# A matrix product by 15 products in place of 11 per two chunks, and one list that orders all engines

## The chip, the cores and the metric

The kernel runs on one core of one Trainium2 chip. The metric is the device time in microseconds (us) of one execution; lower is better. One core has five engines that run side by side, each through its own instructions in order: TensorE (PE, matrix products; its weight loads are listed apart as PEld), VectorE (DVE), ScalarE (ACT), GpSimd (POOL) and SyncE (SP, which here only issues DMAs).

## What is computed

```python
# x: (8, 4096, 192), weight: (8 heads, 7 taps)
w = exp(weight - max) / sum                # softmax over the taps
out[b, s, h, :] = sum_k w[h, k] * x_padded[b, s + k, h, :]   # causal, 6 zeros ahead
X = out.reshape(32768, 192)
h = X @ w_in                               # w_in:  (192, 2048)
g = h * sigmoid(h)                         # SiLU
result = g @ w_out                         # w_out: (2048, 192)
```

All is fp32 (the weights arrive as float64 and are rounded in the kernel). Nearly all arithmetic is in the two products, h and the result.

## The kernel before, in words

The 32768 tokens are worked in 32 blocks of 1024 tokens, each in two halves of 512 (n = 0, 1). Data lie transposed, channels on partitions, tokens along the free dimension. The 192 channels are three thirds of 64; the 2048 columns of `w_in` are 16 chunks of 128. A product of one third of the channels, one chunk and one token half is a matmul with 64 rows: it takes half of the PE array, so two such matmuls, one on the upper rows and one on the lower, run at once. I call the time of such a pair a slot. Block 0 is worked by plain products (`up_plain`, `down_plain`) while the weights are prepared; blocks 1 to 31 use schemes that save products.

**h, blocks 1 to 31 (`product`, line 476 on).** The 16 chunks form 8 pairs m. For a pair, two thirds of the channels and two token halves make eight ordinary products; a Strassen-like scheme does them with seven (P1 to P7), of differences of the tokens (`win`, line 429 on, four per block, on DVE) and of sums of the weights (`combine_in`, on POOL, once). The last third of the channels adds four plain ones (E11, E12, E21, E22). That is 11 of 64 rows for a pair, 88 for a block: 44 slots. The products accumulate in three PSUM banks per pair (`"1"`, `"b"`, `"d"`). Bank `"1"` grows by one product at a time, and its value on the way is copied out (`s1`, `s3` on ACT, `s2` on DVE, line 512), so that the next product onto it waits for the copy. DVE then adds a copy and another bank into g (C11, C22, C12, line 521), and ACT takes SiLU (lines 516 and 518).

**The result (`sum_g`, `out_slot`, `merge`, `turn_out`).** A seven-product scheme over channel halves and token halves. `sum_g` (line 538) makes four differences of g for each j of four, 16 DVE instructions of 1024 columns per block; `out_slot` (line 570) issues four matmuls of 128 rows by 32 columns at once, 48 times per block, eight of them only 128 columns wide: 42 slots' worth. `merge` (lines 630 to 650) puts the six accumulators together, `turn_out` transposes and stores.

**The convolution.** For the next block, DVE transposes the input (`turn_in`, line 387) and does seven taps for each of three thirds (`conv`, lines 406 and 409). `spread` copies each third by DMA to both halves of the partitions (`dup`), where the matmuls read it.

**What sets the order.** The string `PLAN` is written out by hand or by a planner outside the kernel: entries between bars are slots, tokens name instructions (P, E products; s, C, g sums and SiLU; v conv taps; t sums of g; w differences of tokens; M, x, y, z merging; a minus sign means the previous block). `pin` keeps every engine's instructions in the order of issue. In the plan before, 44 slots are all h, then come the slots of the result (`down`), so a block has a stage of h and a stage of the result. PSUM has eight banks, handed out by a pool.

Of the kernel before, what the change touches and what calls it, by code (L numbers as in the profile page):

```python
# [17 lines left out]
def kernel(  # L18
# [54 lines left out]
    upool = ctx.enter_context(tc.tile_pool(name="up", bufs=13))  # L73
# [8 lines left out]
        "P1.0 P1.1 -x1.0 -M4.0 | P1.2 P5.0 -M5.0 s1.1 -M7.0 | P5.1 E22.0 s1.0 -o.1 s1.2 | "  # L82
        "E22.1 P6.1 -o.2 | P6.0 P1.3 s2.1 | P6.2 P5.2 -o.3 s1.3 s2.0 | P5.3 P7.1 s2.2 | "
        "P7.0 E22.2 i.0 s3.1 | P7.2 P6.3 i.1 s3.0 C22.1 | E22.3 E21.1 s3.2 s2.3 | "
        "P4.0 P4.1 g22.1 C22.0 | E12.1 P7.3 C22.2 g22.0 | E21.0 E12.0 i.2 C21.1 s3.3 | "
        "E21.2 E12.2 C21.0 C22.3 | P3.1 P3.0 g22.2 | P4.2 P4.3 g22.3 C12.0 | "
        "E12.3 P2.0 C12.1 g12.0 | P2.1 E11.0 v.00 C21.2 v.01 g12.1 | E11.1 E21.3 C11.0 | "
        "P1.4 P1.5 v.02 C21.3 | P1.6 P3.2 g11.0 C11.1 s1.4 | P3.3 P5.4 C12.2 s1.5 | "
        "P6.4 E22.4 s1.6 C12.3 g11.1 | P5.5 P6.5 s2.4 g12.2 | E22.5 P1.7 v.03 g12.3 s2.5 | "
        "P7.4 P2.2 s1.7 v.04 | P6.6 E11.2 s3.4 v.05 | P2.3 P7.5 C22.4 | "  # L90
        "P4.4 P6.7 s2.6 s3.5 C11.2 | E11.3 E12.4 g22.4 s2.7 g11.2 | P7.6 E21.5 C22.5 | "
        "E21.4 P7.7 C11.3 s3.6 | P3.5 P4.5 v.06 g22.5 s3.7 t.00 | E21.6 P3.4 C21.4 | "
        "E12.5 P4.7 C21.5 t.01 | P4.6 P2.4 g11.3 C12.4 | P5.7 E11.4 C21.6 C12.5 | "
        "E22.7 E21.7 g12.4 C11.4 g12.5 | P2.5 P5.6 C22.7 C21.7 | E11.5 E22.6 t.03 g11.4 | "
        "E12.7 P2.6 g22.7 C22.6 | P3.7 E11.6 C11.5 g22.6 | P2.7 E12.6 t.02 g11.5 | "
        "E11.7 P3.6 C11.6 | C12.7 g11.6 | C11.7 g12.7 C12.6 | g11.7 v.10 g12.6 | v.11 | "
        "v.12 | v.13 v.14 | v.15 | v.16 | t.10 | . | t.11 | . | . | t.13 | v.20 t.12 | . | "
        "v.21 | v.22 | v.23 | v.24 v.25 | v.26 | t.20 | . | . | t.21 | . | t.23 | t.22 | "
        "t.30 | . | t.31 | w.0 | t.32 | . | t.33 | . | w.1 | w.2 | z1.0 w.3 | y0.0 | y1.0 | "
        ". | y2.0 M1.0 | M2.0 | M6.0 | x0.0 | M3.0 x2.0 | o.0"  # L100
# [19 lines left out]
    def load(b, ks=range(NK)):  # L120
        if b not in nats:
            nats[b] = xpool.tile([P, NK, TB // SQ, SQ], F32, tag="nat", name="nat")
        nat = nats[b]
        for k in ks:
            for i in range(P // SQ):
                c = R * k + SQ * (i % 2)
                queue = nc.scalar if not b and k == 0 and i % 2 == 0 else nc.sync
                ins = queue.dma_start(
                    out=nat[SQ * i : SQ * i + SQ, k, :, :],
                    in_=x_v[2 * b + i // 2][:, :, c : c + SQ],  # L130
                )
                if not b:
                    pin(ins)
# [175 lines left out]
    def combine_in(j):  # L309


        s, r = ws[j], wr[j]
        comb(s[:, 1, 0, :], s[:, 1, 0, :], s[:, 1, 1, :], ALU.add)
        comb(s[:, 0, 0, :], s[:, 0, 0, :], s[:, 1, 0, :], ALU.subtract)
        comb(s[:, 0, 0, :], s[:, 0, 0, :], s[:, 0, 1, :], ALU.add)
        comb(s[:, 1, 1, :], s[:, 0, 2, :], s[:, 1, 2, :], ALU.subtract)
        comb(r[:, 0, 1, :], r[:, 1, 0, :], r[:, 1, 1, :], ALU.add)
        comb(r[:, 0, 1, :], r[:, 0, 1, :], r[:, 0, 0, :], ALU.subtract)
        comb(r[:, 1, 0, :], r[:, 0, 0, :], r[:, 1, 0, :], ALU.subtract)
# [58 lines left out]
    def turn_in(b, k):  # L378
        if k == 0 and b:
            xt = xts[b] = xpool.tile([P, NK, pad + TB], F32, tag="xt", name="xt")  # L380
            if b * TT % S == 0:
                nc.gpsimd.memset(xt[0:R, :, 0:pad], 0.0)
            else:
                nc.gpsimd.tensor_copy(xt[0:R, :, 0:pad], tails.pop(b))
        xt = xts[b]
        pin(
            nc.vector.transpose(
                xt[:, k, pad : pad + TB], nats[b][:, k, :, :].rearrange("p k c -> p (k c)")
            )
        )  # L390
        if k == NK - 1:
            if b:
                nc.sync.dma_start(out=xt[R:P, :, 0:pad], in_=xt[0:R, :, TB : TB + pad])
            if (b + 1) * TT % S:
                tails[b + 1] = xpool.tile([R, NK, pad], F32, tag="tail", name="tail", bufs=2)
                nc.sync.dma_start(out=tails[b + 1], in_=xt[R:P, :, TB : TB + pad])
# [16 lines left out]

    def spread(b, k):

        if b not in dups:
            dups[b] = xpool.tile([P, 2, NK, TB], F32, tag="dup", name="dup")
        src = nats[b][:, k, :, :].rearrange("p k c -> p (k c)")
        for n in range(2):
            for e in range(2):  # L420
                nc.sync.dma_start(
                    out=dups[b][R * e : R * e + R, n, k, :], in_=src[R * n : R * n + R, :]
                )
# [3 lines left out]
    def win(b, i):  # L427

        d = dups[b]
        if i == 0:  # L430
            wins[b] = xpool.tile([P, 4, TB], F32, tag="win", name="win")
        t = wins[b]
        u, v = (
            (d[:, 1, 0, :], d[:, 0, 0, :]),
            (d[:, 1, 1, :], t[:, 0, :]),
            (d[:, 1, 1, :], d[:, 1, 0, :]),
            (d[:, 0, 1, :], t[:, 1, :]),
        )[i]
        pin(nc.vector.tensor_tensor(t[:, i, :], u, v, op=ALU.subtract))
# [35 lines left out]
    def product(b, m, name):  # L475
        d, t = dups[b], wins[b]
        e, r, s = m % 2, wr[m // 2], ws[m // 2]

        other, bn, w, v = {
            "P1": (0, "1", r[:, 0, 0, :], d[:, 0, 0, :]),  # L480
            "P6": (0, "1", r[:, 0, 1, :], t[:, 1, :]),
            "P7": (0, "1", r[:, 1, 0, :], t[:, 2, :]),
            "P4": (0, "1", r[:, 1, 1, :], t[:, 3, :]),
            "E21": (0, "1", r[:, 1, 2, :], d[:, 0, 2, :]),
            "P2": (1, "b", s[:, 0, 1, :], d[:, 0, 1, :]),
            "E11": (1, "b", s[:, 0, 2, :], d[:, 0, 2, :]),
            "P5": (1, "d", s[:, 1, 0, :], t[:, 0, :]),
            "E22": (1, "d", s[:, 1, 2, :], d[:, 1, 2, :]),
            "P3": (1, "d", s[:, 0, 0, :], d[:, 1, 1, :]),
            "E12": (1, "d", s[:, 1, 1, :], d[:, 1, 2, :]),  # L490
        }[name]
        half = e ^ other
        first = (b, m, bn) not in bk
        if first:
            bk[b, m, bn] = bank()
        pin(
            nc.tensor.matmul(  # L497
                bk[b, m, bn], rows(w, half), rows(v, half), start=first, stop=True,
                skip_group_check=True,
# [3 lines left out]
    def g_of(b, m, a, n):  # L503
        return g_tile(b, m // 2, a)[:, n, m % 2, :]

    def sums_h(b, name, m):


        if name[0] == "s":
            u = us[b, m, name[1]] = upool.tile([P, TB], F32, tag="u", name="u")  # L510
            copy = nc.vector.tensor_copy if name == "s2" else nc.scalar.copy
            pin(copy(u, bk[b, m, "1"]))  # L512
            return
        g = g_of(b, m, int(name[1]) - 1, int(name[2]) - 1)
        if name == "C21":
            pin(nc.scalar.activation(g, bk[b, m, "1"], AF.Silu))
        elif name[0] == "g":
            pin(nc.scalar.activation(g, g, AF.Silu))  # L518
        else:
            i, bn = {"C11": ("1", "b"), "C22": ("3", "d"), "C12": ("2", "d")}[name]  # L520
            pin(nc.vector.tensor_tensor(g, us.pop((b, m, i)), bk[b, m, bn], op=ALU.add))  # L521

    def sum_g(b, j, i):
# [14 lines left out]
        pin(nc.vector.tensor_tensor(t[i // 2][:, i % 2, :], u, v, op=ALU.subtract))  # L538

    def out_slot(b, j, i, e, half=None):  # L540
# [4 lines left out]
        g = [gs[b, j, a] for a in range(2)]  # L545
        w, x_ = wo[j], wx[j]
        at = 6 if i == 3 and half else i
        if at not in accs.setdefault(b, {}):
            accs[b][at] = bank()

        def t(k):
# [4 lines left out]
            1: lambda: (a_[0][0], g[0][:, 0]),  # L556
            2: lambda: (a_[0][1], g[1][:, 0]),
            3: lambda: (x_[:, 2], g[1][:, 1]),
# [6 lines left out]
        for q in range(4):  # L565
# [8 lines left out]
                    start=j == 0 and e == 0,  # L574
                    stop=j == NJ - 1 and e == 1,
# [3 lines left out]

    def down(b, j):  # L580

        for i in (0, 1, 2, 4, 3, 5) if j < NJ - 1 else (0, 1, 2, 3, 5, 4):
            for e in range(2):
                for half in range(2) if i == 3 and b == NB - 1 else (None,):
                    out_slot(b, j, i, e, half)
                yield
        for a in range(2):
            del gs[b, j, a]
# [324 lines left out]
```

## Time and profile before

The time is 2409.25 us (median of 3 runs, 2409.24 to 2409.34). The profiled execution spans 2407.7 us.

| | us |
|---|---|
| PE busy | 2400.0 of 2407.7 |
| DVE busy | 2062.1 |
| ACT busy | 994.2 |
| POOL busy | 71.0 |
| start until block 1 (plain products, weights) | 101.4 |
| h of one block (176 matmul records) | 37.97 |
| result of one block (384 records) | 36.22 |

An fp32 matmul leaves two records in the trace, one for each pass, so 88 products are 176 records. "Busy" of an engine is the union of its instructions' time; the mean duration of a group is that of one instruction from its start to its end, and consecutive DVE or ACT instructions overlap a little, so that two of them in a row start closer together than one lasts. A wait is shown as idle time before an instruction, with the engine and line that ended it. The chain that ended last is followed back from the last instruction of the program and tells which engine set the end.

### The profile page before, as it was taken

Reading aid. Unit: us, or ns where it says so; the run is one execution under the profiler, and the core shown is the slowest. Engines: PE = TensorE matmul, PEld = TensorE weight load, DVE = VectorE, ACT = ScalarE, POOL = GpSimd, SP = SyncE. Lnnn points to the kernel's source line nnn. Section 1 sums busy time; section 2 is a strip of 40 time slices with the busy share of each in tenths; the row PEclk is TensorE's granted clock in tenths of the full one; section 3 lists DMA queues with packets and bytes.
Section 4 is the critical chain, followed back from the end, with each engine's and each line's share of the span. In section 5 each row is a group of like instructions: output and inputs, shape, how many; then the busy total and the mean of one; then the engine's idle time right before and its main releaser. Section 6 shows DMA issues by size and latency. Waiting matters only on the chain.

```text
span 2407.7 us, 43335 instructions
## 1 busy us (share of the span) xinstructions
PE 2400.0 (100%) x17878; PEld 942.8 (39%) x17878; DVE 2062.1 (86%) x2812; ACT 994.2 (41%) x1873; POOL 71.0 (3%) x99
## 2 busy tenths in 40 slices
PE   9999999999999999999999999999999999999998
PEld 4333443334433344433344333443334433334433
DVE  8789888888888898888988888888889888898876
ACT  4334543334533345433454334453334533345432
POOL 4300000000000000000000000000000000000000
PEclk9999999999999999999999999999999999999999
DMA  7322122221222222222222222122222222222220
GB/s 160 60 45 47 34 36 54 54 41 32 44 46 54 40 41 36 45 54 44 45 37 36 54 51 43 32 39 51 53 41 40 36 45 54 43 43 37 38 40 14
DMA packets 453718, 110.59 MB, mean 46 GB/s; under 512 B 424080, under 2 KB 429200, under 8 KB 453520
## 3 DMA queue, kind: packets, MB, share of 16 engines
q1 hardware_dynamic: 449872, 105.85, 24.0%
q8 instruction: 140, 2.29, 0.4%
q0 software_dynamic: 448, 1.58, 0.3%
q10 hardware_dynamic: 3200, 0.39, 0.1%
q14 instruction: 58, 0.48, 0.1%
HBM read 31.46 MB, written 25.17 MB: 24 GB/s over the span
## 4 chain that ended last, share of the span: by engine, by line
PE 100%; DVE 0%; ACT 0%; issue 0%; ACTq 0%
PE ps L497 49%; PE ps L570 47%; PE ps L599 2%; PE ps L460 2%; PE ps L805 1%; PE ps L339 0%; DVE cmb L111 0%; ACT u L111 0%; DVE osb L111 0%; PE ps L365 0%; ACTq L739 0%; DVE zeros L111 0%; DVE warm L111 0%; ACTq L111 0%
## 5 line engine op out<-in xcount | busy, mean ns | idle before, releaser
L497 PE MATMUL ps<-dup,ws 64*128 64x512 f32 x2480 | 869.9, 589 | 0.0
L570 PE MATMUL ps<-g,wo 128*32 128x512 f32 x2976 | 661.8, 593 | 0.0
L521 DVE TENSOR_TENSOR g<-u,ps 128x512 f32<-128x512 f32 x744 | 486.1, 681 | 119.2 <-PE ps L497 89.8
L497 PE MATMUL ps<-win,wr 64*128 64x512 f32 x1488 | 567.7, 589 | 0.0
L570 PE MATMUL ps<-t,wo 128*32 128x128 f32 (+2 forms) x4528 | 500.6, 446 | 0.0
L518 ACT ACTIVATE g<-g 128x512 f32<-128x512 f32 x744 | 444.6, 630 | 97.3 <-DVE g L521 97.3
L497 PEld LDWEIGHTS ps<-dup,ws 64*128 64x128 f32 x2480 | 363.3, 187 | 291.8 <-issue 277.7
L570 PE MATMUL ps<-t,wx 128*32 128x512 f32 x2976 | 452.7, 592 | 0.0
L409 DVE SCALAR_TENSOR_TENSOR nat<-xt,taps,nat 128x512 f32<-128x512 f32 x564 | 423.4, 751 | 18.3 <-ACT nat L404 3.7
L497 PE MATMUL ps<-dup,wr 64*128 64x512 f32 x992 | 420.0, 596 | 0.0
L512 ACT COPY u<-ps 128x512 f32<-128x512 f32 x496 | 277.7, 588 | 229.3 <-PE ps L497 226.2
L638 ACT COPY cmb<-ps 96x512 f32<-96x512 f32 x30 | 17.4, 581 | 805.3 <-PE ps L570 805.3
L538 DVE TENSOR_TENSOR t<-g 128x1024 f32<-128x1024 f32 x248 | 299.9, 1220 | 27.2 <-PE ps L570 27.2
L538 DVE TENSOR_TENSOR t<-g,t 128x1024 f32<-128x1024 f32 x248 | 303.2, 1223 | 13.6 <-PE ps L570 3.2
L497 PEld LDWEIGHTS ps<-win,wr 64*128 64x128 f32 x1488 | 233.6, 187 | 175.3 <-issue 147.0
L570 PEld LDWEIGHTS ps<-t,wo 128*32 128x32 f32 x4528 | 180.4, 110 | 219.7 <-issue 199.5
L497 PE MATMUL ps<-win,ws 64*128 64x512 f32 x496 | 242.2, 589 | 0.0
L570 PE MATMUL ps<-g,wx 128*32 128x512 f32 x1488 | 234.6, 592 | 0.0
L570 PEld LDWEIGHTS ps<-t,wx 128*32 128x32 f32 x2976 | 121.9, 110 | 278.8 <-issue 269.5
L650 DVE TENSOR_TENSOR cmb<-cmb,ps 96x512 f32<-96x512 f32 x150 | 102.2, 682 | 135.2 <-ACT u L635 133.1
L497 PEld LDWEIGHTS ps<-dup,wr 64*128 64x128 f32 x992 | 160.6, 187 | 128.1 <-issue 114.2
L570 PEld LDWEIGHTS ps<-g,wo 128*32 128x32 f32 x2976 | 168.6, 110 | 98.3 <-issue 98.3
(72 smaller groups left out, 1225.6 us busy)
## 6 DMA issues: line engine op xcount, KB each, us to landing
dup<-nat SPq DMA_DIRECT2D x376, 128.0 KB, 2.3
nat<-in_x_dram SPq DMA_DIRECT2D x382, 64.0 KB, 2.4
out_dram<-osb SPq DMA_DIRECT2D x376, 64.0 KB, 2.0
raw<-in_moe_w_out_dram SPq DMA_DIRECT2D x8, 384.0 KB, 3.9
raw<-in_moe_w_in_dram SPq DMA_DIRECT2D x12, 192.0 KB, 4.7
ws<-wr POOLq DMA_DIRECT2D x8, 192.0 KB, 4.3
raw<-in_moe_w_in_dram SPq DMA_DIRECT2D x6, 128.0 KB, 3.3
xt<-xt SPq DMA_DIRECT2D x31, 4.5 KB, 1.9
```

The source lines that it names most:

```text
L409: nc.vector.scalar_tensor_tensor(out=dst, in0=src, scalar=tap, in1=dst, op0=ALU.mult, op1=ALU.add)
L460: nc.tensor.matmul(hs[a, n, e], rows(wr[j], e)[:, a, k, :], rows(d, e)[:, n, k, :], start=k == 0, stop=k == NK - 1,)
L497: nc.tensor.matmul(bk[b, m, bn], rows(w, half), rows(v, half), start=first, stop=True, skip_group_check=True,)
L512: pin(copy(u, bk[b, m, "1"]))
L518: pin(nc.scalar.activation(g, g, AF.Silu))
L521: pin(nc.vector.tensor_tensor(g, us.pop((b, m, i)), bk[b, m, bn], op=ALU.add))
L538: pin(nc.vector.tensor_tensor(t[i // 2][:, i % 2, :], u, v, op=ALU.subtract))
L570: nc.tensor.matmul(accs[b][at][SQ * q : SQ * q + SQ, to], lhs[:, e, SQ * k : SQ * k + SQ], rhs[:, e, ts(q, TB // 4) if i == 5 else to], st ...
L599: nc.tensor.matmul(acc[k][R * n : R * n + R, :], wo[j][:, a, e, R * k : R * k + R], gs[b, j, a][:, n, e, :], start=j == 0 and a == 0 and e ...
L638: pin(nc.scalar.copy(c[0], acc[0][0:n, :]))
L650: pin(nc.vector.tensor_tensor(out_, u, v, op=ALU.add))
L805: nc.tensor.matmul(by_pe[k][n], rows(diag, n)[:, k, i, :], rows(xts[0], n)[:, k, i : i + TB], start=i == 0, stop=i == K - 1,)
```

## The change

For h, three chunks are taken together with all three channel thirds and both token halves: 18 ordinary products become 15. Five groups of three chunks cover 15 of the 16 chunks; the sixteenth is done plainly (`plain`, three products of 64 rows for one token half, six of half the columns for the other). So a block has 75 + 3 + 3 = 81 half-array products of 512 columns in place of 88. In a group, products run in three chains of accumulation, each on one bank: (5, 2, 6, 1, 0, 14), (3, 9, 7, 4, 8) and (12, 10); 13 and 11 are added by PE onto banks that DVE wrote. The first chain's value is copied out by ACT (`u`) after five of its six products; DVE makes two sums from PSUM into PSUM (`X`), three into g (`a`) and two corrections in place (`b`); ACT does SiLU of six (`S`). The differences of tokens become six (`win`), the sums of weights 98 POOL instructions on 64 partitions (`combine`), where 28 on 128 partitions were.

All orders of a block come from one list, `PLAN`, with 129 entries; it starts in the middle of the result of the block before, and mixes products of h (P, L), result slots (D) and all work of the other engines and the DMA issues (`ld`, `sp`, `st`). Token tiles, dup, win and the eight PSUM banks are fixed and used again by every block. In the part of the list that is mostly h, the products of two groups alternate. The purpose is to do the same work with fewer matmuls and with the other engines' work spread evenly beside PE.

```diff
-    upool = ctx.enter_context(tc.tile_pool(name="up", bufs=13))
+    upool = ctx.enter_context(tc.tile_pool(name="up", bufs=10))
...
+        "P5.0 | -P8.3 ld.1 -t.20 | -D2.10 -t.21 | -D4.11 ld.2 | -D3.10 -w.0 -a0.3 | -D5.11 | "
...
+        "-D4.31 -M2.0 | -D5.31 | -D3.30 -x2.3 -x2.2 -y1.0 | P2.0 | L.02 -M3.0 -y2.0 -w.5 | "
+        "-D4.30 u4.0 -M6.0 -x0.0 | P6.0 | P3.0 -M4.0 v.12 | L.00 | P5.4 u2.0 X2.0 | L.01 | "
+        "P1.0 u5.4 v.03 | P9.0 | P2.4 SL.0 -M5.0 -x2.0 -x2.1 | L.10 v.04 u0.0 | L.11 -o.1 "
+        "-x1.0 | L.12 u4.4 | P0.0 | P13.0 X4.0 SL.2 -M7.0 | P12.0 | P6.4 u1.0 v.20 | P3.4 | "
+        "P14.0 b1.0 u2.4 S2.0 v.21 | P1.4 | P7.0 S3.0 X2.4 | P11.0 | P10.0 a5.0 | P5.1 | "
+        "P9.4 S4.0 b5.0 u0.4 | P4.0 | P13.4 X4.4 u5.1 v.13 | P12.4 | P0.4 a1.0 | P2.1 | P7.4 "
+        "u1.4 -o.2 | P11.4 | P8.0 b1.4 u4.1 -st.2 a5.4 S5.0 | P14.4 | P6.1 S2.4 a0.0 | P10.4 "
+        "| P4.4 -o.3 u2.1 S3.4 | P3.1 -st.3 | P1.1 a1.4 S4.4 | P5.2 X2.1 | P8.4 u0.1 -st.1 "
+        "b5.4 | P9.1 | P0.1 u5.2 a0.4 -o.0 | P12.1 | P2.2 u1.1 X4.1 -st.0 | P13.1 | P14.1 "
+        "u4.2 v.05 | P7.1 | P6.2 b1.1 S2.1 S3.1 | P3.2 | P11.1 a5.1 u2.2 S0.4 | P4.1 | P10.1 "
...
+        "P8.2 | P14.3 v.25 | P4.3 | P10.3 sp.0 t.01 | D1.31 a0.2 | D1.21 t.03 S0.2 | D1.10 "
+        "S3.3 S5.2 t.10 | D2.01 | D2.00 v.16 | D4.01 a1.3 sp.1 b5.3 | D3.00 v.26 S5.3 | "
+        "D0.20 S1.3 t.11 sp.2 | D4.00 | D3.01 t.12 | D1.30 +ld.0 t.13 | D5.00 | D2.11 | "
+        "D5.01"
...
+    def combine(g, e):
+
+        def op(sign, to, u, v):
+            comb(raw(g, *to, e), raw(g, *u, e), raw(g, *v, e), ALU.add if sign > 0 else ALU.subtract)
...
+        for order in COMBINE[e]:
+            op(*order)
...
+        if i == 0:
+            sub(t(0), d(0), d(1))
+        elif i == 1:
+            sub(t(1), t(0), d(2))
+        elif i == 2:
+            add(t(2), t(1), d(3))
+        elif i == 3:
+            add(t(3), t(2), d(5))
+        elif i == 4:
+            sub(rows(t(4), 1), rows(t(0), 1), rows(t(3), 1))
+        else:
+            sub(rows(t(4), 0), rows(d(4), 0), rows(t(3), 0))
...
+    ON_B = (0, 1, 2, 4, 5, 6, 11, 14)
+    CHAINS = ((5, 2, 6, 1, 0, 14), (3, 9, 7, 4, 8), (12, 10))
+    def chain_bank(g, c):
+        return banks[(c * 2 + QUEUE.index(g) % 2) if c < 2 else 4]
...
+        if r in (13, 11):
+            to, first = banks[XBANK[2 if r == 13 else 4]], False
+        else:
+            c = next(c for c in range(3) if r in CHAINS[c])
+            to, first = chain_bank(g, c), r == CHAINS[c][0]
...
+        if name[0] == "u":
+            us[b, g, o] = upool.tile([P, TB], F32, tag="u", name="u")
+            pin(nc.scalar.copy(us[b, g, o], t1))
+        elif name[0] == "X":
+            add(banks[XBANK[o]], us.pop((b, g, o)), t2)
+        elif name[0] == "a":
+            add(h_of(b, g, o), us.pop((b, g, o)), t2)
+        elif name[0] == "b":
+            c = us.get((b, g, o), None)
+            c = h_of(b, g, o) if c is None else c
+            add(c, c, t3, ALU.subtract)
...
+    banks = [bank() for _ in range(8)]
+    begun = set()
+    for b in range(1, NB + 2):
+        for s in plan:
+            for t in s:
+                step(b, t)
```

In a token such as P6.1 the first number is the product and the second the group; the groups come in the order 0, 4, 1, 2, 3. In D2.10 the 2 is the accumulator, then come j and half of the rows.

## The prediction

> **What bounds the kernel now.** I read the page's busy line first, then its chain, then that chain in order of time.
>
> ```profile
> PE 2400.0 (100%) x17878; PEld 942.8 (39%) x17878; DVE 2062.1 (86%) x2812; ACT 994.2 (41%) x1873; POOL 71.0 (3%) x99
> ...
> PE 100%; DVE 0%; ACT 0%; issue 0%; ACTq 0%
> ```
>
> ```profile
> 1214.16 37.97 PE ps L497 x176
> 1252.13 36.22 PE ps L570 x384
> 1288.34 37.97 PE ps L497 x176
> ```
>
> PE never stops: a block is 37.97 + 36.22 = 74.19 us, the same for every block. A slot (two half-array products side by side, or one result slot) is 37.97 / 44 = 0.863 us, and in the result stage 36.22 / 42 = 0.862. So 31 blocks are 2299.9 us; the start (101.4) and the tail (about 6.4) are the rest of the span.
>
> The busy time by stage, for one block (columns: span, PE, PEld, DVE, ACT, POOL busy with counts, clock, DMA share, GB/s):
>
> ```profile
> 1214.16:1252.13 37.97, 37.97 (x180) 16.96 (x184) 33.26 (x51) 24.77 (x46) 0.00 (x0) 1.00 0.15 22
> 1252.13:1288.34 36.21, 36.21 (x386) 12.05 (x386) 30.94 (x38) 6.08 (x13) 1.07 (x1) 1.00 0.34 67
> ```
>
> DVE is busy 33.26 + 30.94 = 64.20 us of 74.19: 10.0 us of idle time, the second engine by far. DMA and POOL are no candidates in steady state. The groups by form give the prices:
>
> ```profile
> L521 DVE TENSOR_TENSOR g<-u,ps 128x512 f32<-128x512 f32 x744 | 486.1, 681 | 119.2 <-PE ps L497 89.8 <-ACT u L512 23.0
> ...
> L538 DVE TENSOR_TENSOR t<-g 128x1024 f32<-128x1024 f32 x248 | 299.9, 1220 | 27.2 <-PE ps L570 27.2
> ...
> L512 ACT COPY u<-ps 128x512 f32<-128x512 f32 x496 | 277.7, 588 | 229.3 <-PE ps L497 226.2
> ...
> L439 DVE TENSOR_TENSOR win<-dup 128x512 f32<-128x512 f32 x62 | 42.4, 685 | 0.0
> ```
>
> The timeline gives a latency that PE does not feel today but will matter:
>
> ```profile
> 1219.32 1.25 DVE L512 COPY u<-ps 128x512 f32<-128x512 f32 x2
> ...
> 1220.02 0.18 PEld L497 LDWEIGHTS ps<-win,wr 64*128 64x128 f32 x1 [0.48 <-DVE u L512]
> ...
> 1220.21 0.59 PE L497 MATMUL ps<-dup,ws 64*128 64x512 f32 x1
> ...
> 1220.64 0.59 PE L497 MATMUL ps<-dup,ws 64*128 64x512 f32 x1
> ...
> 1221.26 0.58 ACT L512 COPY u<-ps 128x512 f32<-128x512 f32 x1 [0.23 <-PE ps L497]
> ```
>
> A product has its two passes at 1220.21 and 1220.64, and the copy of its bank starts at 1221.26: 1.05 us after the product's start. The copy lasts 0.58. The first of the two DVE copies ends near 1219.97, and the weight load that waits for it starts 0.05 later and lasts 0.18. Product, copy, next product on the same bank: 1.05 + 0.58 + 0.05 + 0.18 = 1.86 us at the least, 2.16 slots. The plan before leaves three slots or more there, so the wait ends in time and PE stays full.
>
> **What the Trainium skill says.** "TensorE: Matmul & The Clock Gate", Part 3: Packing small matmuls, says that matmuls on different row groups run at once; the trace agrees: 88 half-array products take 44 slots. "PSUM — Partial Sum Buffer", PSUM bank collisions raise a hardware error, says accesses of two engines to one bank must be guarded by semaphores: so each product of a chain waits for the copy or sum before it, as the load at 1220.02 does. "VectorE: DVE Perf Modes", The perf-mode tier table, says fp32 tensor_tensor runs at one element a cycle, from SBUF or PSUM; the trace agrees, 681 ns with a PSUM operand and 685 without. "SBUF — State Buffer", Who interferes with whom, says that a DVE instruction with two SBUF inputs contends with a GpSimd instruction that reads SBUF; in the start of this trace the same 768-column DVE step takes about 0.95 us with POOL quiet and 1.1 to 1.2 beside it.
>
> **The change part by part.**
>
> *PE, removed.* 88 products become 81: 3.5 slots of 0.863 = 3.0 us per block. I checked the list: products of the upper and lower rows come in pairs and no result slot splits a pair, so the list is 40.5 + 42 = 82.5 slots, 71.2 us against 74.19. Over 31 blocks: -92.7 us, if PE stays full.
>
> *PE, added waits.* The first chain now has six products on one bank with a copy after each of the first five, and the list often sets them two slots apart. In group 1: P2.1, P6.1, P1.1, P0.1, P14.1 are each two slots (four passes, 1.72 us) after the one before, and need 1.86. Each is thus 0.14 us late even with ACT at once free, and PE's queue stands behind it: behind P6.1 stand P10.4, P4.4, P3.1, and for these wait ACT (u2.1) and DVE (a1.4). There are 14 such pairs in a block's first chains. I walked the stretch from P2.0 to P10.3 in issue order with 1.05 us to the reader, 0.58 for a copy, 0.60 from one DVE sum to the next, 0.66 for a tap and 0.23 back to PE: nine places add (P6.0, P1.0, P14.0, P6.1, P1.1, P0.1, P14.1, P0.2, P1.3), the others are covered by delay already taken. Nine times 0.14 to 0.15, with some sharing, is 1.4 us per block. Bounds: 0 if the result is usable sooner than I read, and 2.8 if all 14 and the four places of the second chain below (0.21 each) add up. I take 1.4.
>
> *DVE, added.* Sums 7 x 5 = 35 in place of 4 x 8 = 32, differences 6 in place of 4: five more. In a run of such sums the second starts 0.60 after the first, so +3.0 us: 67.2 us of a block. Against 71.2 + 1.4 that is 93%, and every sum is now on a path to a product: X before P9 and P7, a5 before P4, a1 before P8. The second chain leaves two slots in four places (P9.1, P4.1, P8.4, P9.2) and a DVE sum lasts 0.65, so these need 1.93. In my walk the sum is just in time there, e.g. P4.1 after a5.1. The list spreads DVE evenly: by six slots (5.2 us) its entries come to 3.5 to 5.9 us. The X sums write PSUM, which no row here shows: between 0.58 (no difference) and 0.75, the longest 512-column DVE step in the trace (a tap); I take 0.60. For lateness of DVE beyond my walk I add 0.3 us per block, bounds 0 and 3.
>
> *ACT.* 16 copies become 25 and 32 SiLU become 30 and a plain one in three pieces: 9 x 0.59 = +5.3 us on 24.77 + 6.08, half of a block. It costs time only by the latency above.
>
> *Result stage.* Its DVE work (16 steps of 1.14 to 1.22 us) now runs with the buffers of three t tiles as before. t.12 waits for D4.00, and t.13 after it must be done for D4.11, 5.5 slots after D4.00's end: two steps, 2.4 us of 4.7. No stall.
>
> *SP, buffers.* Tiles used again by name, separate stores and loads: nothing, they lie in the DMA's idle time (share 0.15 to 0.34). The dup copies land in 2.3 us and the list gives the nearest reader, P5.0, some 7 slots.
>
> *Start.* POOL has 98 sums of weights in place of 28. The trace's 128-column sums take 0.66 to 1.34 each:
>
> ```profile
> 30.16 5.36 POOL L307 TENSOR_TENSOR ws<-ws 128x128 f32<-128x128 f32 x4 [6.16 <-DMA ws<-wr]
> ...
> 43.08 2.64 POOL L307 TENSOR_TENSOR ws<-ws 128x128 f32<-128x128 f32 x4 [4.16 <-DMA ws<-wr]
> ...
> 68.69 6.45 POOL L307 TENSOR_TENSOR wr<-wr 128x128 f32<-128x128 f32 x7
> ```
>
> At 0.92 they are 90 us, from 30 on: until about 120 to 135 with the result's weights between. Block 1 begins near 101, but its later groups start 11 to 24 us later, so most hides. POOL also slows the taps of block 1, which end at 93 now, by some 20% of 14 us, and two more differences follow. I add 6 us once, bounds 0 and 14 in this case.
>
> Sum: period 71.2 + 1.4 + 0.3 = 72.9 us, 1.29 less than 74.19. 31 x 1.29 = 40.0. 2409.25 - 40.0 + 6 = 2375 us.
>
> **The rivals.**
>
> *A, PE stays full.* The list hides the round trips, or results are read sooner. For it: it is made from measured durations, and PE has no stall today at all. Against: 1.86 is more than 1.72 in 14 places. 71.2 per block: 2409.25 - 92.7 + 6 = 2322 us (2317 with a free start).
>
> *B, DVE becomes the bound (slower).* DVE has 67.2 us and stands in order, so a wait for PE or ACT in one chain delays the sums of all. Today it idles 10.0 us a block, of which 119.2 / 31 = 3.8 is waiting with a g sum. If it keeps 7.8 us of idle time, the period is 75.0: 2409.25 + 31 x 0.81 + 6 = 2440 us. For it: more sums are on the way back to PE, and idle time must fall to 5.7 for my forecast. Against: the even spread, and the merging that causes some of today's idle time (3.76 us before the first sum of a merge) is moved.
>
> *C, the start.* If the small POOL sums take 1.34 us, the 98 take 131 us, and groups 2 and 3 of block 1 wait some 25 to 30 us: 2375 + 25 = 2400 us. Against: POOL's 1.34 is seen in one run of four only.
>
> **How the numbers follow.** Forecast 0.48, A 0.20, B 0.20, C 0.12. Faster by over 0.2% means below 2404.4: A, nearly all of the forecast, most of C: 0.75. Within 0.2%: the upper edge of the forecast and of C, 0.05. Slower: B, 0.20. The range leaves out the far part of B: low 2318 (A with a short start), high 2430.
>
> **What would show it.** PE's h products become 81 per block and the chain still mostly PE: the counting is right. PE or weight loads waiting on `u` of ACT, 0.1 to 0.2 us each, nine or so times a block: the forecast. A period of 71.2: A. A chain that runs through DVE sums, and DVE above 93%: B. A gap of PE between 101 and 135 us, ended by POOL: C. I am wrong if waits on X, a or b exceed those on u, or if X takes clearly over 0.75.

## The result and the profile after

The changed kernel takes 2419.34 us (2416.69 to 2420.95), the kernel before beside it 2409.3: a ratio of 1.004, 95% interval 1.0026 to 1.0054. It is slower by 0.4%, where 2375 was forecast. It lies inside the range of the prediction, 2318 to 2430, but in the part that was given to rival B, and the trace below does not show B's cause: that the range holds is luck.

The page of the changed kernel, busy times and the chain that ended last:

```profile
PE 2389.8 (99%) x17630; PEld 981.6 (41%) x17630; DVE 2138.2 (88%) x2967; ACT 1147.8 (47%) x2183; POOL 114.1 (5%) x169
...
PE 94%; DVE 3%; SPq 1%; issue 1%; DMA 1%; ACT 0%; DVEq 0%; ACTq 0%
```

PE still sets the end, and it is busy nearly all the time. So the loss isn't a new bound. It lies where "busy" does not show it, or at one place. The same chain in order of time, for a block and a bit (start, us, what):

```profile
...
1230.73 1.00 PE ps L683 x8
...
1258.31 1.85 PE ps L683 x16
...
1281.13 1.06 PE ps L579 x4
...
```

L683 are result slots, L579 the products of h. Before, a block had one piece of each. Now there are five of each (the left-out lines hold the others), and the short ones are too long for what they hold: one result slot (eight records) lasts 1.00 us and not 0.862, two last 1.85, and one pair of products (four records) 1.06 and not 0.863.

One period of that chain (columns as in the table by stage of before):

```profile
1214.00:1287.70 73.70, 73.70 (x556) 30.05 (x552) 66.53 (x93) 35.80 (x68) 1.07 (x1) 1.00 0.23 42
```

The period is 73.70 us, the same in all undisturbed blocks: 0.49 less than 74.19, where 1.29 less was forecast. Over 31 blocks that is -15.2 us. The time rose by 10.1, so 25.3 us were lost outside the period. The view of PE's waits (us in total, times, longest) has 17.2 of them in one piece, at the start:

```profile
PE ps L579 <- DVE ps L611: 17.2, 1, 17.2
```

This wait has a second price. While PE stood still, its granted clock fell to 0.50, and it stayed there for the first 6.02 us after the wait (columns as before; the third number from the end is the clock):

```profile
125.67:131.69 6.02, 6.02 (x20) 3.57 (x22) 2.43 (x4) 0.97 (x2) 0.00 (x0) 0.50 0.01 3
```

In this stretch passes of 512 columns follow each other by some 0.86 us (126.68 and 127.54, for one); later, at a clock of 1.00, by 0.43. So about 3 us more are lost there, an estimate: half of 6.02. In the kernel before the clock is 1.00 all through this stretch. The rest of the 25.3, some 5 us, was not taken apart.

Prices of the new work, from the page's costliest groups:

```profile
L615 ACT COPY u<-ps 128x512 f32<-128x512 f32 x775 | 450.4, 586 | 211.0 <-PE ps L579 196.6
...
L611 DVE TENSOR_TENSOR ps<-u,ps 128x512 f32<-128x512 f32 x310 | 214.2, 691 | 58.9 <-ACT u L615 26.0
```

The copy lasts 0.586 us as forecast, and a sum that writes PSUM (`ps<-u,ps`) 0.691, hardly more than the 0.681 of a sum into SBUF. DVE has 66.53 us in a block (67.2 were forecast). Those terms were right.

**Two readings of the trace that the experiments then test.** The first is a change from products to a result slot and back, in the timeline (start, us, engine, line, operation, tiles; in brackets the idle time before it and what ended it):

```profile
1229.61 0.69 PE L579 MATMUL ps<-win,wr 64*128 64x512 f32 x1
...
1230.14 0.59 PE L579 MATMUL ps<-win,wr 64*128 64x512 f32 x1
...
1230.66 0.12 PEld L683 LDWEIGHTS ps<-t,wx 128*32 128x32 f32 x3 [0.76 <-issue]
1230.66 0.63 PE L683 MATMUL ps<-t,wx 128*32 128x512 f32 x3
...
1231.12 0.60 PE L683 MATMUL ps<-t,wx 128*32 128x512 f32 x3
...
1231.67 0.69 PE L579 MATMUL ps<-win,wr 64*128 64x512 f32 x1
...
1232.20 0.59 PE L579 MATMUL ps<-win,wr 64*128 64x512 f32 x1
```

The tile form in the line changes from `64*128` to `128*32` and back. In a steady stretch the passes follow each other by 0.43 us. Here the distances are 0.53, 0.52, 0.46, 0.55, 0.53; the next is 0.42 again. In a steady stretch a weight load starts a pass ahead of its matmul; at 1230.66 both start together. By such distances the way to the result slots costs about 0.12 us and the way back about 0.21.

The second is the tight round trip of a chain, which the forecast had priced at 1.86 us. P2.1, its copy, and P6.1 on the same bank:

```profile
1243.82 0.59 PE L579 MATMUL ps<-win,ws 64*128 64x512 f32 x1
...
1244.87 0.58 ACT L615 COPY u<-ps 128x512 f32<-128x512 f32 x1 [0.22 <-PE ps L579]
...
1245.50 0.18 PEld L579 LDWEIGHTS ps<-win,ws 64*128 64x128 f32 x1 [0.21 <-ACT u L615]
1245.53 0.67 PE L579 MATMUL ps<-win,ws 64*128 64x512 f32 x1
...
1246.04 0.59 PE L579 MATMUL ps<-win,ws 64*128 64x512 f32 x1
```

From product to product it is 1245.53 - 1243.82 = 1.71 us, two slots to within 0.01. The late weight load shows only in the second pass, 0.51 behind the first in place of 0.43: the delay is 0.08, not 0.14. There are some fourteen such late loads in a block, behind copies and sums, at 0.05 to 0.11 each.

### The profile page after: what moved, and what is told of

Read it like the earlier page. It is cut to its first block, busy times and chain, and to the rows that moved or that the text cites. A ratio compares the mean times of both kernels' runs of the same rounds, so it can differ in the third digit from the quotient of the medians.

```text
span 2417.5 us, 43655 instructions
## 1 busy us (share of the span) xinstructions
PE 2389.8 (99%) x17630; PEld 981.6 (41%) x17630; DVE 2138.2 (88%) x2967; ACT 1147.8 (47%) x2183; POOL 114.1 (5%) x169
## 4 chain that ended last, share of the span: by engine, by line
PE 94%; DVE 3%; SPq 1%; issue 1%; DMA 1%; ACT 0%; DVEq 0%; ACTq 0%
PE ps L683 47%; PE ps L579 45%; PE ps L591 2%; DVE two L123 1%; DVE nat L457 1%; DVE mh L123 0%; DMA nat<-in_x_dram 0%; SPq L140 0%; SPq L772 0%; DMA dup<-nat 0%; DVE t L123 0%; SPq L474 0%; DVE wo L123 0%; DVE xt L425 0%; DMA xt<-xt 0%
## 5 line engine op out<-in xcount | busy, mean ns | idle before, releaser
L579 PE MATMUL ps<-win,ws 64*128 64x512 f32 x1550 | 704.1, 610 | 17.9 <-DVE ps L611 17.2
L683 PE MATMUL ps<-g,wo 128*32 128x512 f32 x2976 | 708.7, 594 | 0.0
L579 PE MATMUL ps<-win,wr 64*128 64x512 f32 x1550 | 656.5, 609 | 1.1 <-DVE win L491 1.1
L615 ACT COPY u<-ps 128x512 f32<-128x512 f32 x775 | 450.4, 586 | 211.0 <-PE ps L579 196.6
L683 PE MATMUL ps<-t,wo 128*32 128x512 f32 (+2 forms) x4528 | 543.6, 446 | 0.0
L683 PE MATMUL ps<-t,wx 128*32 128x512 f32 x2976 | 491.7, 594 | 0.1
L627 ACT ACTIVATE g<-g 128x512 f32<-128x512 f32 x465 | 279.1, 628 | 438.9 <-DVE g L611 438.9
L579 PE MATMUL ps<-dup,wr 64*128 64x512 f32 x868 | 411.8, 594 | 0.0
L579 PE MATMUL ps<-dup,ws 64*128 64x512 f32 x682 | 345.7, 603 | 0.0
L579 PEld LDWEIGHTS ps<-win,wr 64*128 64x128 f32 x1550 | 234.5, 186 | 235.5 <-issue 87.4
L611 DVE TENSOR_TENSOR g<-u,ps 128x512 f32<-128x512 f32 x465 | 314.3, 681 | 15.0 <-PE ps L579 14.1
L579 PEld LDWEIGHTS ps<-win,ws 64*128 64x128 f32 x1550 | 240.4, 186 | 177.7 <-DVE ps L611 68.8
L627 ACT ACTIVATE g<-ps 128x512 f32<-128x512 f32 x465 | 263.6, 596 | 56.5 <-PE ps L579 56.5
L683 PEld LDWEIGHTS ps<-t,wo 128*32 128x32 f32 x4528 | 179.2, 110 | 239.3 <-issue 228.6
L611 DVE TENSOR_TENSOR ps<-u,ps 128x512 f32<-128x512 f32 x310 | 214.2, 691 | 58.9 <-ACT u L615 26.0
L683 PE MATMUL ps<-g,wx 128*32 128x512 f32 x1488 | 246.8, 595 | 0.0
L683 PEld LDWEIGHTS ps<-t,wx 128*32 128x32 f32 x2976 | 115.5, 110 | 269.4 <-issue 267.9
L683 PEld LDWEIGHTS ps<-g,wo 128*32 128x32 f32 x2976 | 162.0, 110 | 135.4 <-issue 135.4
```

What stands on the lines that cost most here:

```text
L579: nc.tensor.matmul(to, raw(g, *LEFT[e][r], e), rhs, start=first, stop=True, skip_group_check=True)
L611: pin(nc.vector.tensor_tensor(out_, u, v, op=op))
L615: pin(nc.scalar.copy(us[b, g, o], t1))
L627: pin(nc.scalar.activation(h, src, AF.Silu))
L683: nc.tensor.matmul(accs[b][at][SQ * q : SQ * q + SQ, to], lhs[:, e, SQ * k : SQ * k + SQ], rhs[:, e, ts(q, TB // 4) if i == 5 else to], st ...
```

## The experiments

Two theories stand against each other for the 31 blocks. **Changes:** each pair of changes between the two tile forms costs 0.33 us, and the list has five pairs per block where one was. **Chains:** the products of a chain wait for copies and sums. For the start: SyncE's order, POOL, or DVE's order. Each kernel ran beside the kernel before on the same chip.

### Changes put into the kernel before

```diff
-| P2.7 E12.6 t.02 g11.5 | E11.7 P3.6 C11.6 | C12.7 g11.6 | C11.7 g12.7 C12.6 |
+| t.02 g11.5 | C11.6 | P2.7 E12.6 C12.7 g11.6 | E11.7 P3.6 g12.7 | C11.7 C12.6 |
```

The 45th and later slots of that list stand behind a result slot each. The two moved pairs read the token tile when the next block's tokens are already being laid into it, so their values aren't the reference's; number, form and size of the instructions are those of the kernel before.

> The kernel before with one edit: the last two pairs of half-array products of a block stand behind the first and the second result slot, in place of ahead of all; nothing is added or left out. The row then changes three times per block from products to result slots and back, in place of once. Theory 1 (TensorE loses 0.33 us at each such pair of changes, 0.115 on the way to the result slots and 0.215 back): 2 x 0.33 x 31 = 20.5 us more than 2409.3, about 2430. Rival (a change costs nothing; the changed kernel loses only by waits for copies and sums in its chains): 2409 to 2411, since TensorE waits for nothing in the kernel before and these products' sums are needed only by the last result slots.

Measured: 2430.0 us against 2409.6, +20.4. The chain in order of time:

```profile
1224.19 36.25 PE ps L495 x168
1260.44 0.99 PE ps L568 x8
1261.44 1.06 PE ps L495 x4
...
1299.05 1.05 PE ps L495 x3
```

A result slot between products lasts 0.99 and a pair of products between result slots 1.06, as in the changed kernel, though nothing waits for data here. The period is 1299.05 - 1224.19 = 74.86, 0.67 more than 74.19: 0.335 per pair of changes. The theory of changes is shown, with its price. What it is in the change that costs, the form itself or the four smaller weight loads that come with it, these runs do not separate.

### Two more changes in the changed kernel

```diff
-| D0.11 S1.0 b1.2 S5.4 | P3.3 | P6.3 t.00 S0.1 |
+| P3.3 | P6.3 t.00 S0.1 | D0.11 S1.0 b1.2 S5.4 |
...
-| D0.21 S2.3 t.02 | P8.2 | P14.3 v.25 |
+| P8.2 | P14.3 v.25 | D0.21 S2.3 t.02 |
```

One difference of g (t.00) now reads a tile before its SiLU (S1.0), so values differ there.

> The changed kernel with one edit: of the two places where two result slots stand between products, each is split, so that one pair of products stands between the two slots: two changes and back more per block, seven pairs in place of five. Theory 1 (0.33 us per pair of changes): 2 x 0.33 x 31 = +20.5 us, about 2440. Rival (only the waits for copies and sums in the chains cost): the distances in the chains stay or shrink by one slot at one product with four slots in reserve, so 2418 to 2421.

Measured: 2447.6, +28.3, more than either theory said. The period is 74.60, +0.90. From slot to slot, the two new pairs of changes take 0.66 of it. The other 0.24 is mostly one late product, P1.3. The edit carried the SiLU S1.0 behind t.00, a DVE step of 1.22 us that reads the same tile: ACT stands 0.87 us waiting for it (in the trace at 1276.25), so the copy u2.3 behind it ends late, and P1.3 starts 0.22 behind P10.2, where it was 0.02. 31 x 0.66 = 20.5 is the part that the theory of changes named; the rest is a flaw of the edit, and shows what one copy late in ACT's queue costs.

### One change fewer

```diff
-| D1.01 b1.3 S1.2 a5.3 S4.3 | D0.21 S2.3 t.02 | P8.2 | P14.3 v.25 | P4.3 | P10.3 sp.0 t.01 |
+| b1.3 S1.2 a5.3 S4.3 | S2.3 t.02 | P8.2 | P14.3 v.25 | P4.3 | P10.3 sp.0 t.01 | D1.01 | D0.21 |
```

> The changed kernel with one edit: the two result slots D1.01 and D0.21, which stand between products of the last group, stand behind the last product P10.3: four pairs of changes per block in place of five. Theory 1 (the changes are all that these slots cost): one pair less, -0.33 x 31 = -10 us from 2419.3, about 2409. Theory 2 (these slots also give a1.2, a5.3 and u1.3 the time to end; without them P8.2 and P14.3 stand waiting): P8.2 follows P7.3 and the sums by 1.7 us less, and the wait of about 0.8 us outweighs the change: some 0.5 us more per block, +15 us, about 2435.

Measured: 2432.7, +13.4; period 74.06, +0.36. In the timeline P8.2 stands waiting for DVE, and 1.2 us later P4.3 does so again (0.89):

```profile
1275.17 0.18 PEld L577 LDWEIGHTS ps<-win,wr 64*128 64x128 f32 x1 [1.27 <-DVE g L609]
```

So the result slots between the products are not idle splitting: they give the sums time, at 0.335 us per place. Here, taking a change away without putting products in its place lost more than it saved. Theory 2 of that run holds, on top of the price of the change.

### Shorter copies

```diff
-            pin(nc.scalar.copy(us[b, g, o], t1))
+            n = TB if o == 1 else TB // 2
+            pin(nc.scalar.copy(us[b, g, o][:, 0:n], t1[:, 0:n]))
...
-            add(banks[XBANK[o]], us.pop((b, g, o)), t2)
+            add(cut(banks[XBANK[o]]), two(us.pop((b, g, o))), cut(t2))
```

(`two` gives the first 256 columns twice, `cut` the same view of a full tile; the sums `a` are changed alike.)

> The changed kernel with one edit: 20 of the 25 u copies per block copy 256 columns in place of 512, and the sums read these 256 twice, so half of what these copies carry is left out; instructions, order and engines are the same. A copy then lasts some 0.38 us in place of 0.586. Theory 1 (beside the changes between products and result slots, 1.2 us per block are lost where weight loads stand behind these copies and the sums after them): the part behind the copies goes, about 0.5 us per block, -15 us from 2419.3, to about 2404. Rival (the loss is in the changes alone, or in VectorE's order): 2417 to 2421.

Measured: 2404.9, -14.4; period 73.22, -0.48. The copies in the groups by form:

```profile
L622 ACT COPY u<-ps 128x256 f32<-128x256 f32 x620 | 230.8, 372 | 206.3 <-PE ps L579 185.9 <-PE ps L591 18.6
```

So 0.48 us per block of the loss does lie behind the ends of these copies, where the forecast had 1.4. What is left lies more with the sums than with the copies: in one block of this run (1224.0 to 1297.2 us) weight loads of h still wait 4.5 us for DVE's sums, in 13 places, and 1.9 us for copies, in four.

### The start, one wait behind another

In the start of the changed kernel, DVE's timeline ahead of the sum X2.0 (`ps<-u,ps`), for which P9.0 and so all of PE waits:

```profile
117.73 1.31 DVE L425 STREAM_TRANSPOSE xt<-nat 128x512 f32<-128x512 f32 x2 [8.29 <-DMA nat<-in_x_dram]
...
124.92 0.69 DVE L611 TENSOR_TENSOR ps<-u,ps 128x512 f32<-128x512 f32 x1
```

DVE stands 8.29 us on the last loads of block 2's input. SyncE's queue shows why: the last three are issued behind twelve stores.

```profile
107.69 6.35 SPq L772 DMA_DIRECT2D out_dram<-osb  x12
114.08 1.58 SPq L140 DMA_DIRECT2D nat<-in_x_dram  x3
```

First edit:

```diff
+    did.update((0, t) for t in base if t[0] not in "ivw")
+    for k in (0, 1, 2):
+        step(1, f"ld.{k}")
     for k in range(NK):
         turn_out(0, k)
         store_out(0, k)
-    did.update((0, t) for t in base if t[0] not in "ivw")
-    for t in (t for s in plan for t in s if t[0] == "+"):
-        step(0, t)
```

> The changed kernel with one edit: the twelve loads of block 2's input are issued on SyncE ahead of the twelve stores of block 0's result (the last four of them stood behind the stores). Theory 1 (the start is late because the loads stand behind the stores, so VectorE stands 8.3 + 2.1 us on the transpose and first tap of block 2's last third, and with it the sum that the second chain waits for): most of the 17.2 us that TensorE waits for a VectorE sum goes away, and the time falls by 15 to 20 us from 2419.3, to 2399 to 2404. Rival (the start is late because POOL's 98 weight sums and the taps beside them are slow): nothing of this is touched, 2417 to 2420.

Measured: 2419.9. My reading had failed: no gain at all. DVE's first tap came even later, and the wait before it had another name, a copy on POOL:

```profile
122.68 1.19 DVE L454 TENSOR_SCALAR nat<-xt,taps 128x512 f32<-128x512 f32 x2 [12.78 <-POOL xt L442]
```

In POOL's timeline of the same run:

```profile
122.46 0.19 POOL L442 COPY xt<-tail 64x18 f32<-64x18 f32 x1
```

The copy moves 64 rows of 18 elements, the halo of block 2. It takes 0.19 us, but POOL's queue has 98 weight sums and the result's ahead of it, up to 122 us. In the changed kernel it was there too, ending at 120.73, hidden behind the loads. So POOL does cost at the start, as rival C had it, though by a copy in its queue and not by late weights. The second edit puts this copy, for block 2 alone, on ScalarE, with the loads first:

```diff
-            nc.gpsimd.tensor_copy(xt[0:R, :, 0:pad], tails.pop(b))
+            copy = pin_copy if b == 2 else nc.gpsimd.tensor_copy
+            copy(xt[0:R, :, 0:pad], tails.pop(b))
```

> The changed kernel with two edits: the loads of block 2 ahead of the stores (as in the run before), and the copy of block 2's halo columns (64 rows of 18 elements) on ScalarE in place of POOL, where it stood behind the last weight sums and ended at 122.65 us. Theory (the start is late because VectorE's first tap of block 2's last third waits for whichever comes last of the loads and of that POOL copy; the loads alone came first and left the copy): the first tap comes some 10 us earlier and the time falls by 8 to 15 us from 2419.3, to 2404 to 2411. Rival (VectorE's taps slowed by POOL, or TensorE's waits for weight sums, set the start): no change, 2417 to 2420.

Measured: 2414.7, -4.7, below the range that I gave: a third wait appeared.

```profile
115.64 2.35 DVE L458 TENSOR_SCALAR nat<-xt,taps 128x512 f32<-128x512 f32 x2 [5.53 <-DMA xt<-xt]
```

The transfer of the other half's halo (`xt<-xt`) now stood behind the same twelve stores, issued at 113.6. The third edit puts the stores after it (in the trace ten of the twelve are issued behind it) and, in block 1 alone, hands out block 2's taps one by one behind the products from P9.0 on:

```diff
+    for t in (t for s in plan for t in s):
+        if t[0] == "v":
+            held_back.append(t)
+            continue
...
+        free = free or t == "P9.0"
+        n_pe += t[0] in "PDL"
+        if free and t[0] in "PDL" and n_pe % 2 == 0 and held_back:
+            step(1, held_back.pop(0))
```

> The changed kernel with edits at the start alone: loads of block 2 first, its halo copy on ScalarE, the stores of block 0's result after the halo transfer, and in block 1 the taps for block 2 handed out one by one behind the products from P9.0 on, in place of all ahead of the first sum X2.0. Theory (what is left of the start's loss is VectorE's queue: taps that wait for the halo stand ahead of X2.0, and P9.0 waits for X2.0): the 14.7 us that TensorE still waits at 108 us shrink to 2 to 5, and the time falls by 10 us from 2414.7, to 2402 to 2407. Rival (VectorE only pays later, since the same taps must be done before block 2): 2411 to 2415.

Measured: 2405.9, -13.4 from the changed kernel. X2.0 now comes at 109.45 in place of 124.92, and the taps wait behind it:

```profile
109.45 0.66 DVE L615 TENSOR_TENSOR ps<-u,ps 128x512 f32<-128x512 f32 x1
```

The last edit has two parts, and which of them gave the gain was not tried apart. Some 3 us of the 13.4, by the estimate above, come with the clock: PE has no wait over 1.1 us from 95 to 175 us of this run, the clock stays at 1.00, and the slow stretch is gone.

Of the 25.3 us some 12 remain against the kernel before. From 95 to 175 us of this run PE's weight loads wait for POOL's sums (4.1 us in three places) and for DVE sums (11 us in fifteen); which of these is the cause of the 12 was not tried.

### An order that pays both prices knowingly

The same entries of the list in another order, searched for with the measured prices: 0.335 us per pair of changes, 1.05 from a product to its reader, 0.08 behind a copy. It has two pairs of changes per block, and steps of a chain are kept apart by products of other groups.

```diff
-| P2.0 | L.02 | -D4.30 | P6.0 | P3.0 | L.00 | P5.4 | L.01 | P1.0 | P9.0 | P2.4 |
+| L.02 | P2.0 | P5.4 | L.00 | L.01 | P6.0 | P3.0 | P2.4 | L.10 | L.11 | P1.0 | L.12 | P9.0 |
...
-| P2.3 | P12.2 | D0.01 | D0.11 | P3.3 | P6.3 | P11.2 | P7.2 | P10.2 | P1.3 |
+| P2.3 | P13.2 | P1.2 | P3.3 | P6.3 | P12.2 | P0.2 | P7.2 | P11.2 | P9.3 | P1.3 |
...
-| P11.3 | P7.3 | D1.01 | D0.21 | P8.2 | P14.3 | P4.3 | P10.3 | D1.31 |
+| P12.3 | P11.3 | P14.3 | P8.2 | P10.3 | P4.3 | D0.21 | D0.01 | D1.01 |
```

(PE's entries alone; the other engines' entries move with them.)

> The changed kernel with another list: the same entries, in an order searched for with the durations measured here (0.33 us per pair of changes, 1.05 us from a product to its reader, 0.08 us from a copy's end to the product behind it); two pairs of changes per block in place of five, and products of other groups, in place of result slots, between the steps of a chain. Theory 1 (both costs as measured): 0.74 us per block less, -23 us from 2419.3, about 2396. Theory 2 (the changes alone): 3 x 0.33 = 1.0 us per block less, about 2388. Rival (without result slots between the products the chains wait, as in the run with one pair less): 2420 or more.

Measured: 2392.4, between the two theories: -26.9 from the changed kernel, ratio to the kernel before 0.9929 (0.9915 to 0.9942). The chain in order of time:

```profile
1225.43 29.40 PE ps L577 x130
1254.83 16.88 PE ps L681 x168
...
```

The period is 72.75, 0.95 less. Three pairs of changes are 1.0, so what lies behind late loads stayed about as it was. Over 31 blocks the period gives -29.5; some 2.5 us are lost again outside it.

With the edits of the start:

> Both: the list with two pairs of changes, and the edits of the start. Theory (the two are separate costs): -23 and -14 us from 2419.3, about 2382, below the kernel before by 1.1%. Rival (the start's work is only moved, or the list's gain is not real): 2396 or more.

Measured: 2380.0 us, ratio 0.9878 (0.9864 to 0.9891): -39.3 from the changed kernel, where the two gains alone sum to -40.3. They add up to within 1 us, and this kernel beats both. Its start is not free yet: PE waits 4.0 us for a POOL sum there, and the clock stands at 0.50 from 108 to 112 and from 128 to 130 us. Another order, found with the same prices, has three pairs of changes:

> As the run before with a list of three pairs of changes, whose chains have a little more room. Theory 1 (late loads count as in the model): the same period, about 2382. Theory 2 (the model prices late loads too high, as the last runs hint: 74.06 us measured for 74.32): one pair more costs 0.1 to 0.3 us per block, 2385 to 2391.

Measured: 2397.6, worse than either theory. Its period is 73.36, 0.61 more than 72.75: one pair of changes is 0.335 of it. The rest, some 0.28, was not taken apart by a run; in the trace the largest single delay is a load of the plain products, which waits 0.93 us for a SiLU behind two other ACT instructions and lets PE's next pass start 0.26 late. The prices pick out the large terms, but do not rank two orders that lie within half a microsecond.

## Why the prediction was wrong

**The sum, put right.** Slots removed, -92.7 us: right, the trace has 81 products' worth of slots. The period is 73.70 - 71.2 = 2.50 us above a full PE, where 1.7 were forecast. Four more pairs of changes at 0.335 are 1.34 of it. (The 71.2 already holds one pair: it is worked from slots of the kernel before, which has one.) The remaining 1.16 are put down to late loads and waits; the fourteen late loads at about 0.08 come to 1.1. So: -92.7 + 31 x 1.34 + 31 x 1.16 + 25.3 = +10 us, in which 1.16 and 25.3 are what was left over after the measured terms.

**The step that failed first: "no result slot splits a pair, so the list is 82.5 slots".** The sentence is true and the conclusion isn't. The step priced the mixing of products and result slots at nothing. It costs 41.5 us over 31 blocks: four more pairs of changes at the 0.335 that was measured by putting two such pairs alone into the kernel before, and the order with three pairs fewer gave 0.95 per block back. The Trainium skill, "TensorEngine Tiling (Array Packing)", Key Properties, says that changing the tiling mode, and not just the tile, drains TensorE. It gives no figure; the runs agree that such a change costs time and have one, 0.335 us per pair of changes. I had not drawn on that page. The kernel before showed it too: its two stages meet once per block, and I spread that loss over the slots.

**The start: +6 us, in truth about +25.** I looked at POOL's busy time and at the taps. What counted was who stands in which queue: loads and a halo transfer behind stores on SyncE, a 0.19 us copy behind all weight sums on POOL, and DVE's taps ahead of the first sum PE needs. Nor did the forecast ask what PE's clock does in a long wait, about 3 us here. I had priced "separate stores and loads" at nothing, for they "lie in the DMA's idle time". It was the queue that mattered, not the DMA. Rival C named POOL and a gap that POOL ends; the 17.2 us were one gap, ended by DVE, and POOL was the second cause behind it. That C's total for the start, 6 + 25 = 31 us, lies near the measured one is luck.

**The round trips: the copies are there, but are not the larger part.** 1.86 us counted the whole weight load (0.18) ahead of the product. The product's record starts 0.03 behind the load's, so the trip is 1.71, and a late load costs 0.08 in its second pass. For copies 1.4 us per block were forecast, and shortening them gave back 0.48. For lateness of DVE 0.3 were forecast; 1.16 - 0.48 = 0.68 are left for it and for all else. The prediction's own sign of being wrong, waits on X, a or b above those on u, did show. PE's weight loads in one block (1214.0 to 1287.7 us; in total, times, longest) wait longer for sums than for copies:

```profile
PEld ps L579 <- ACT u L615: 2.5, 5, 0.8
PEld ps L579 <- DVE g L611: 2.4, 6, 0.8
PEld ps L579 <- DVE ps L611: 1.9, 5, 0.6
```

Most of this time costs nothing, since PE is busy with earlier passes; how the 0.68 divides between the sums and the rest was not tried. In all, 1.7 us were forecast for waits and 1.16 measured. This miss, 17 us over 31 blocks, was on the other side and hid over a quarter of the two others (41.5 and 19).

**What held.** DVE at 66.53 us per block did not become the bound (rival B): in steady blocks the chain is all PE, and DVE's 3% of it are in the start. X at 691 ns, ACT at half, the buffers of t and the result stage without a stall: right. Rival A, a full PE, was closer to hand than I thought in the chains, but each block paid for the changes.

## What to carry to other kernels

When a planner mixes two kinds of matmul, look at the tile form in the trace's lines: a change from row tiles to column tiles and back had a price here of 0.335 us, two fifths of a slot, and PE looks busy while it is paid. Merging alone is no cure if the pieces between were there to give a round trip time; put other independent products there. At a start, follow each wait one step into the queue of the engine that ends it, and expect the next wait to stand right behind the first: three edits were needed before the time moved by more than 5 us. Then read the clock behind the wait too.

## What the runs showed of the hardware

- A change of tile form delays weight loads and passes although PE's busy time stays at 99%: 0.12 us on the way from 64-row tiles to 32-column tiles, 0.21 on the way back, by the distances of passes; 0.335 together by the time of the kernel before with two more of them.
- A weight load that started only 0.03 us ahead of its matmul cost 0.08 us, in the second pass (0.51 behind the first in place of 0.43).
- After a wait of 17.2 us PE's granted clock was 0.50 for the first 6.02 us of work, with passes of 512 columns some 0.86 us apart in place of 0.43; with no wait over 1.1 us at the start of the run with all three edits it stayed at 1.00.
- POOL's sums on 64 partitions by 128 columns lasted 0.45 us while DVE transposed or stood idle (108 to 115 us of the start), and 0.78 to 0.90 beside DVE's taps and `win` sums (85 to 106 us); what makes the difference was not tried.
